# A two-attention kernel with a list scheduler: first weights through another DMA queue, constants later, smaller staging tiles, more output tiles, and new cost numbers

## The chip, the cores and the metric

The kernel runs on one core of a Trainium2 chip. The metric is the device time of one execution in microseconds (us), lower is better. Every number quoted as a time is the median of a kernel's fast runs; a kernel that is compared was run on the same chip as runs of the kernel before, alternating with them. The "span" of a profile is the time from the first to the last instruction of one profiled execution; it is about 2 us shorter than the time.

## The reference

Two attention layers on separate inputs of 2048 rows and 640 columns, with 32 heads of 20 columns each. The outputs stand side by side.

```python
def A(x, wq, wk, wv, wo, beta):         # 4 segments of 512 rows
    q, k, v = split_heads(x @ wq), split_heads(x @ wk), split_heads(x @ wv)
    g = sigmoid(beta)                   # one gate per head
    for s in range(4):
        p = softmax(qs @ ks.T * scale + causal_mask)      # inside the segment
        a_dot = p @ vs
        a_mem = (phi(qs) @ M) / (phi(qs) @ z + 1e-6)      # memory of earlier segments
        o = g * a_mem + (1 - g) * a_dot
        M, z = M + phi(ks).T @ vs, z + sum(phi(ks))
    return o @ wo                       # phi(t) = t + 1 if t > 0 else exp(t)

def B(x, wqkv, wo):                     # causal, window of 256 rows
    scores = where(0 <= i - j < 256, q @ k.T * scale, -1e9)
    return (softmax(scores) @ v) @ wo
```

## The kernel before

The work is cut into eight chunks of 512 rows, A0, B0, A1, B1, A2, B2, A3, B3. For each chunk there are projections (q, k, V), scores with an exponential on ScalarE, value products, a normalisation on VectorE, and a final projection with `wo`. This document numbers chunks and stages from 0 to 7; stage n runs from the end of the last score exponential of chunk n-1 to that of chunk n, and the tail runs from the end of the last score exponential to the end of the span.

The order of the instructions is fixed while the program is built, by a list scheduler written in Python. Class `Flow` keeps a modelled clock for each engine. A number such as `f.on_dve(607.0)` issues nothing: it only tells the scheduler how long the instruction just issued is believed to take. A changed cost number changes the order of the instructions and nothing else.

```python
class Flow:                                   # modelled clocks, ns
    def on_pe(self, mode, ns, ready=0.0): ...
    def on_dve(self, ns, ready=0.0):
        self.dve = max(self.dve, ready + 100.0) + ns
        return self.dve
    def when_idle(self, t, fn):               # VectorE work for when it is idle by the model
        self.idle_dve.append((t, fn))
...
def close(self, i, t):                        # one of two PSUM banks is free at modelled time t
    self.f.bank_free[i] = t
```

Projections of q and k are "bounced": TensorE's result is copied to a staging tile, stored to scratch memory in DRAM, and spread from there over the partitions of `qA`, `kA`, `qB` or `kB`. phi takes one exponential on ScalarE and two VectorE instructions, which are issued when the model sees VectorE idle.

```python
def qk_job(self, n, what, half, w_ap, scratch, dst, needs):
    ...                                       # 5 matmuls into a bank for each m
        nc.vector.tensor_copy(out=st[:, m, :], in_=ps[:, :])
        t = f.on_dve(615.0, f.pe)
        self.close(bi, t)
        self.bounce(m, st, scratch, dst, t, n, what)
...
def phi(self, out, in_, ready, then):
    e = self.wk.tile([P, L], BF16, name="e", bufs=2)
    nc.scalar.activation(out=e[:], in_=in_, func=ACT.Exp)
    ta = f.on_act(519.0, ready)
    def s1():
        nc.vector.tensor_single_scalar(out=e[:], in_=e[:], scalar=1.0, op=ALU.min)
        f.on_dve(200.0)
    def s2():
        nc.vector.scalar_tensor_tensor(out=out, in0=in_, scalar=0.0, in1=e[:],
                                       op0=ALU.max, op1=ALU.add)
        f.on_dve(650.0)
    f.when_idle(ta + 50.0, s1); f.when_idle(ta + 50.0, s2)
```

The final projection of a chunk loads the stored output transposed and does 8 groups of five matmuls (4 row blocks, two halves of the columns). There are 310 such matmuls in all, called *finals* below; the last row block of B3 goes another way.

```python
def final_job(self, n, o, scr, wo, out2d, r0, col, t0, t1):
    yield t
    yield self.quiet                          # not while a bounce is under way
    ...                                       # store o to scratch
    nc.sync.dma_start_transpose(out=oT[:, :, t0 * P:t1 * P], in_=scr[t0 * P:t1 * P, :])
    for tt in range(t0, t1):
        ot = self.wk.tile([P, 640], BF16, name="ot", bufs=2)
        for hf in range(2):
            yield "bank"
            ...                               # 5 matmuls, a VectorE copy to ot
        ...                                   # store ot to the output
```

The projections of a chunk are seeded as jobs when the scores of the chunk ahead of it begin. For chunk B1 they are seeded in two parts, and the argument `early` says which part takes V along:

```python
self.seed(n + 1, False if n == 2 else None)   # n: chunk whose scores begin now
if n == 1:
    self.seed(3, True)                        # B1's k early; its q follows with early=False
...
if early is not False:                        # in seed(): V goes with k
    add(self.v_job(n, half, *v))
```

The softmax here doesn't subtract the row's maximum and nothing guards it: scores larger than these inputs give would overflow.

## Time and profile before

| | before |
|---|---|
| time, median of 4 fast runs | 402.5 us (400.4 to 404.7) |
| span of the profiled run | 400.8 us |
| ScalarE / TensorE / VectorE busy | 337.7 / 348.7 / 318.7 us |
| first score exponential | 14.4 us |
| last score exponential ends | 383.6 us |
| tail | 17.2 us |

The page of the profile gives the sums (columns of its second line: busy us, share of the span, number of instructions) and, in 40 slices of the span, the granted TensorE clock (the share of full speed at which TensorE ran) in tenths:

```profile
span 400.8 us, 11055 instructions
...
PE 348.7 (87%) x4260; PEld 159.7 (40%) x4260; DVE 318.7 (80%) x654; ACT 337.7 (84%) x396; POOL 268.2 (67%) x552
...
PEclk9999999998999999999999999999999999999699
```

Three engines are busy 80 to 87% of the time, so which of them limits has to be read stage by stage.

The ScalarE timeline (start us, busy us, line, operation, count, and in brackets the idle time before it and what ended that) shows three gaps of the start:

```profile
14.38 5.61 ACT L568 ACTIVATE pt<-sc 128x1024 bf16<-128x1024 f32 x6 [6.89 <-PE sc L556]
...
29.46 20.37 ACT L568 ACTIVATE pt<-sc 128x1024 bf16<-128x1024 f32 x22 [4.11 <-PE sc L556]
...
70.68 18.15 ACT L568 ACTIVATE pt<-sc 128x768 bf16<-128x768 f32 x22 [3.00 <-PE sc L556]
```

The view of waits says that VectorE's copies to the output tile waited four times, 5.8 us in all, for a store to let the tile go:

```profile
DVE ot L784 <- DMA out_dram<-ot: 5.8, 4, 2.2
```

The TensorE timeline of the tail shows how finals run when nothing else is left: one group of five each 0.68 to 0.74 us, and one wait for the last transposed load.

```profile
391.32 0.84 PE L778 MATMUL m_7589<-wo_B,oT 128*128 128x320 bf16 x5
392.06 0.84 PE L778 MATMUL m_7596<-wo_B,oT 128*128 128x320 bf16 x5
395.49 0.85 PE L778 MATMUL m_7607<-wo_B,oT 128*128 128x320 bf16 x5 [2.58 <-DMA oT<-scr_o_216]
```

Finally, the groups of VectorE's instructions by form (busy us, mean ns of one, idle before) give the true length of what the scheduler believes. The trace's mean is after the bar and comma:

```profile
L588 DVE TENSOR_TENSOR pt<-pt,fdmask 128x512 bf16<-128x512 bf16 x64 | 29.9, 467 | 1.5 <-ACT pt L568 1.5
L688 DVE TENSOR_TENSOR u<-tt,rr 128x320 bf16<-128x320 f32 x24 | 15.0, 626 | 1.8
L387 DVE TENSOR_SCALAR e<-e 128x512 bf16<-128x512 bf16 x33 | 12.6, 382 | 0.0
L391 DVE SCALAR_TENSOR_TENSOR stq<-stq,e 128x512 bf16<-128x512 bf16 x15 | 11.8, 788 | 0.3
```

The kernel's numbers for these four are 350, 410, 200 and 650 ns. All are too low. The changed kernel has 440, 540, 300 and 740.

### The profile page before, as it was taken

The numbers are of one execution on the slowest core, as the hardware profiler recorded it, in microseconds if no ns is written. First come the engines' busy times: TensorE is split into PE (matmuls) and PEld (weight loads), VectorE is DVE, ScalarE is ACT, GpSimd is POOL, SyncE is SP. The second block draws the span as 40 slices with busy tenths as digits, with TensorE's granted clock in tenths as the row PEclk, the third lists the DMA queues.
The fourth block names the chain that finished last, engine by engine and source line by source line (L and its number), as shares of the span: only waits on it lengthen the run. The fifth ranks groups of instructions, "written<-read, shape, count | busy, mean of one in ns | idle before, by whom it ended". The sixth has DMA issues, their size and how long they took to land.

```text
span 400.8 us, 11055 instructions
## 1 busy us (share of the span) xinstructions
PE 348.7 (87%) x4260; PEld 159.7 (40%) x4260; DVE 318.7 (80%) x654; ACT 337.7 (84%) x396; POOL 268.2 (67%) x552
## 2 busy tenths in 40 slices
PE   6889999989898787798898988799789987998893
PEld 2334333434433323344443333344443334555462
DVE  6566699568998878977899988987778889988472
ACT  1549991989899998999999998999979998999820
POOL 5226660898867777988676786988756877756520
PEclk9999999998999999999999999999999999999699
DMA  7965255885438725152653925062526322237482
GB/s 170 283 255 175 74 139 146 196 205 140 104 101 208 149 86 127 48 150 88 150 110 115 231 84 136 13 165 80 154 73 167 96 70 69 77 108 147 107 179 83
DMA packets 101653, 52.67 MB, mean 131 GB/s; under 512 B 71712, under 2 KB 101536, under 8 KB 101536
## 3 DMA queue, kind: packets, MB, share of 16 engines
q1 hardware_dynamic: 101456, 51.88, 50.2%
q8 instruction: 33, 0.54, 0.6%
q14 instruction: 20, 0.16, 0.1%
q10 hardware_dynamic: 144, 0.08, 0.1%
HBM read 18.19 MB, written 23.10 MB: 103 GB/s over the span
## 4 chain that ended last, share of the span: by engine, by line
PE 35%; DVE 34%; ACT 10%; POOL 8%; DMA 6%; issue 6%; SPq 1%; ACTq 0%; DVEq 0%
ACT pt L568 10%; DVE tt L658 8%; PE sc L556 6%; POOL pt L606 4%; DVE o L688 3%; DVE st L367 3%; DVE ot L784 3%; DMA out_dram<-ot 2%; POOL pt L603 2%; DVE e L387 2%; PE m_73 L246 2%; DMA pkT<-scr_pk_197 2%; DVE stk L391 2%; DVE stq L391 2%; DVE rr L676 2%
## 5 line engine op out<-in xcount | busy, mean ns | idle before, releaser
L568 ACT ACTIVATE pt<-sc 128x1024 bf16<-128x1024 f32 (+1 forms) x360 | 322.4, 1016 | 34.1 <-PE sc L556 33.1
L606 POOL TENSOR_SCALAR_AFFINE_SELECT pt<-pt 128x256 bf16<-128x256 bf16 (+1 forms) x336 | 176.8, 536 | 107.4 <-ACT pt L568 105.3
L603 POOL TENSOR_SCALAR_AFFINE_SELECT pt<-pt 128x256 bf16<-128x256 bf16 x160 | 76.1, 479 | 7.7 <-ACT pt L568 7.4
L688 DVE TENSOR_TENSOR o<-tt,rr 128x320 bf16<-128x320 f32 x64 | 37.9, 592 | 1.9
L778 PEld LDWEIGHTS <-oT 128*128 128x128 bf16 x310 | 27.8, 98 | 25.7 <-issue 10.6
L556 PE MATMUL sc<-qA,kA 32*128 32x128 bf16 (+3 forms) x512 | 36.2, 301 | 2.1 <-ACT pt L568 1.6
L511 PEld LDWEIGHTS <-xT 128*128 128x128 bf16 x320 | 25.7, 97 | 27.7 <-issue 13.7
L588 DVE TENSOR_TENSOR pt<-pt,fdmask 128x512 bf16<-128x512 bf16 x64 | 29.9, 467 | 1.5 <-ACT pt L568 1.5
L556 PE MATMUL sc<-qB,kB_128 32*128 32x128 bf16 (+2 forms) x416 | 27.4, 270 | 1.8 <-ACT pt L568 1.8
L556 PE MATMUL sc<-qB,kB_129 32*128 32x128 bf16 (+1 forms) x480 | 25.1, 246 | 4.2 <-ACT pt L568 4.1
L556 PEld LDWEIGHTS <-kA 32*128 32x128 bf16 x512 | 10.9, 91 | 38.5 <-issue 36.6
L696 POOL TENSOR_TENSOR o<-o,u 128x320 bf16<-128x320 bf16 x24 | 19.6, 817 | 0.0
L556 PEld LDWEIGHTS <-kB_128 32*128 32x128 bf16 x416 | 10.0, 92 | 21.8 <-issue 20.4
L619 PEld LDWEIGHTS <-vA 128*32 128x32 bf16 x512 | 11.0, 96 | 18.3 <-DVE st L367 5.2
L556 PEld LDWEIGHTS <-kB_129 32*128 32x128 bf16 x480 | 10.5, 94 | 17.9 <-issue 16.9
L688 DVE TENSOR_TENSOR u<-tt,rr 128x320 bf16<-128x320 f32 x24 | 15.0, 626 | 1.8
L676 DVE RECIPROCAL rr<-tt 128x16 f32<-128x16 f32 x64 | 14.9, 234 | 0.3
L361 PEld LDWEIGHTS <-wBq 128*128 128x128 bf16 x100 | 8.8, 97 | 13.2 <-issue 5.3
L361 PEld LDWEIGHTS <-wBk 128*128 128x128 bf16 x100 | 8.5, 97 | 12.2 <-issue 4.9
L387 DVE TENSOR_SCALAR e<-e 128x512 bf16<-128x512 bf16 x33 | 12.6, 382 | 0.0
L391 DVE SCALAR_TENSOR_TENSOR stq<-stq,e 128x512 bf16<-128x512 bf16 x15 | 11.8, 788 | 0.3
L361 PEld LDWEIGHTS <-wq_A 128*128 128x128 bf16 x75 | 6.4, 97 | 10.9 <-issue 5.9
(666 smaller groups left out, 627.0 us busy)
## 6 DMA issues: line engine op xcount, KB each, us to landing
out_dram<-ot SPq DMA_DIRECT2D x31, 160.0 KB
wBk<-in_B_wqkv_dram SPq DMA_DIRECT2D x1, 800.0 KB
wBq<-in_B_wqkv_dram SPq DMA_DIRECT2D x1, 800.0 KB
wBv<-in_B_wqkv_dram SPq DMA_DIRECT2D x1, 800.0 KB
scr_wo_A<-in_A_wo_dram SPq DMA_DIRECT2D x4, 200.0 KB
wo_A<-scr_wo_A SPq DMA_DIRECT2D x1, 800.0 KB
scr_wo_B<-in_B_wo_dram SPq DMA_DIRECT2D x4, 200.0 KB
wo_B<-scr_wo_B SPq DMA_DIRECT2D x1, 800.0 KB
```

The lines of the kernel that those rows point to most:

```text
L361: nc.tensor.matmul(ps[:, :], lhsT=w_ap[:, kt, m * P:(m + 1) * P], rhs=xT[:, kt, :], start=(kt == 0), stop=(kt == self.KT - 1))
L391: nc.vector.scalar_tensor_tensor(out=out, in0=in_, scalar=0.0, in1=e[:], op0=ALU.max, op1=ALU.add)
L511: nc.tensor.matmul(ps[:, nw * x:nw * (x + 1)], lhsT=xT[:, kt, tt * P:(tt + 1) * P], rhs=w_ap[:, kt, DH * h0:DH * h0 + nw], start=(kt == 0) ...
L556: nc.tensor.matmul(ps[j // 2][:, j % 2, c0:c0 + nq * P], lhsT=k[rows, g, P * kc:P * kc + P], rhs=q[rows, g, q0 * P:(q0 + nq) * P], start=T ...
L568: nc.scalar.activation(out=pt[:, :, lo:hi], in_=ps[i][:, :, lo:hi], func=ACT.Exp, scale=self.scale)
L588: nc.vector.tensor_tensor(out=pt[:, :, 0:256], in0=pt[:, :, 0:256], in1=self.fd[:].unsqueeze(1).to_broadcast([P, 2, 256]), op=ALU.mult)
L603: nc.gpsimd.affine_select(out=blk, in_=blk, pattern=pat, compare_op=ALU.is_ge, fill=self.zero, base=-1, channel_multiplier=1)
L606: nc.gpsimd.affine_select(out=blk, in_=blk, pattern=pat, compare_op=ALU.is_ge, fill=self.zero, base=0, channel_multiplier=-1)
L658: self.nc.vector.transpose(out=tt[:, :], in_=O[:, :])
L676: nc.vector.reciprocal(out=rr[:], in_=src)
L688: nc.vector.tensor_tensor(out=to, in0=a, in1=b, op=ALU.mult)
L778: nc.tensor.matmul(ps[:, 0:320], lhsT=oT[:, m, tt * P:(tt + 1) * P], rhs=wo[:, m, 320 * hf:320 * hf + 320], start=(m == 0), stop=(m == sel ...
```

## The change

The intent has several parts. The first pieces of the first two weights and the gate `beta` are loaded through ScalarE's DMA queue instead of SyncE's. The gate constants leave VectorE's first path. Loads and stores on SyncE's queue wait, with a patience, while a bounce is under way. Chunks of B use five staging tiles of one piece each instead of two tiles of five pieces, and the output has four tiles instead of two. V of chunk B1 is projected with its q instead of with its early k (below: the *early flip*). And fourteen cost numbers of the scheduler are raised towards what instructions really take (below: the *cost numbers*). The diff, cut to its core (cuts are marked with dots; the comments in it are mine):

```diff
-        def part(i):
+        def part(i, eng=self.nc.sync):
...
-        part(0)
+        part(0, eng or self.nc.sync)                 # eng = ScalarE for wk_A and wq_A
...
-    def quiet(self):
+    def quiet(self, patience):
         f = self.f
-        return None if f.bouncing else max(0.0, f.sp)
+        end = f.pe + patience
+        return lambda: end if f.bouncing else max(0.0, min(f.sp, end))
...
-        t = f.on_dve(607.0, f.pe)                    # eviction of A0's k and q
+        t = f.on_dve(700.0, f.pe)
...
-        self.st[(n, what)] = self.st_tile("st" + what) if n % 2 == 0 else self.wk.tile(
-            [P, self.KT, L], BF16, name="st", bufs=2)
+        self.st[(n, what)] = self.st_tile("st" + what) if n % 2 == 0 else None
...
-            nc.vector.tensor_copy(out=st[:, m, :], in_=ps[:, :])
-            t = f.on_dve(615.0, f.pe)
+            to = st[:, m, :] if n % 2 == 0 else self.wk.tile([P, L], BF16, name="st", bufs=5)[:]
+            nc.vector.tensor_copy(out=to, in_=ps[:, :])
+            t = f.on_dve(670.0, f.pe)
...
-            f.on_dve(200.0)                          # phi, first instruction
+            f.on_dve(300.0)
-            f.on_dve(650.0)                          # phi, second instruction
+            f.on_dve(740.0)
...                                                   # more such: memory update 700 -> 1100,
...                                                   # V 75 + 1.04 n -> 120 + 1.08 n, mask 350 -> 440,
...                                                   # POOL mask 130 + 114 r -> 220 + 110 r,
...                                                   # transpose 640 -> 700, add 75 -> 220,
...                                                   # reciprocal 165 -> 210, multiply 410 -> 540,
...                                                   # POOL add 450 -> 750, final copy 405 -> 440
-        ot = self.wk.tile([P, 640], BF16, name="ot", bufs=2)
+        ot = self.wk.tile([P, 640], BF16, name="ot", bufs=4)
...
-            if early is not False:
+            if early is not True:
                 add(self.v_job(n, half, *v))
...
-        f.pe = f.act = 7000.0
+        f.pe = f.act = 4500.0
...
-            add(self.job(self.proj_direct(0, self.wk_A, self.xs[0], self.kA, g, "k", 6800.0)))
-            add(self.job(self.proj_direct(0, self.wq_A, self.xs[0], self.qA, g, "q", 6900.0)))
-            if g in (1, 5):
+            add(self.job(self.proj_direct(0, self.wk_A, self.xs[0], self.kA, g, "k", 5000.0)))
+            add(self.job(self.proj_direct(0, self.wq_A, self.xs[0], self.qA, g, "q", 5100.0)))
+            if g in (2, 5):
...
-        late = [self.consts_beta, self.consts_gates]
+        late = [self.consts_gates]                   # and only after 35 us instead of 12
...
-                n, g, what = pend[0]                 # value product or memory product
+                x = 0                                # skip memory products whose M is not ready
+                while x < len(pend) - 1 and pend[x][2] == "mem" and self.done.get(
+                        ("dm", chunks[pend[x][0]][1] - 1), 1e12) > f.pe:
+                    x += 1
+                n, g, what = pend[x]
```

## The prediction

> **What bounds it now.** By the page, ScalarE is busy 337.8 us of a 400.8 us span; TensorE 348.7, VectorE 318.7. The ScalarE timeline places the other 63 us: about 13 before its first exponential (14.4 us), 5.7 in two gaps (20.0 to 29.5), about 9 between 61 and 70.7, about 15 in some twenty gaps from 70 to 335, about 17 after its last exponential (383.6). So ScalarE bounds the middle, with TensorE and VectorE close behind, but not start and tail.
>
> **What the change does, by place.** Read from the built instruction order of both kernels.
>
> 1. First weights on ScalarE's queue: worth almost nothing. The first projection starts at 10.81 us, right behind 24 warm-up matmuls (3.13 to 10.75 us), which stay. First exponential still near 14.4.
> 2. Constants off the first path: VectorE's beta and gate constants, 16.85 to 20.0 us, delay V's evictions and stall TensorE 1.8 us; groups 2's q and k now also precede V. The gaps at 20 and 25 us mostly close. B's first scores stand about ten projection matmuls (2 us) earlier, and the qB spread no longer queues behind the 2 us of pk stores. First B score: 70.2 to about 65.5 us. Gain 5.
> 3. Four output tiles remove VectorE's 5.8 us of waits for output stores. ScalarE was covered for most of it: gain 2.
> 4. New order in the middle: all 310 final-projection matmuls move behind the first seven score stages (before, 120 ran within them), freeing about 17 us of TensorE and 11 us of VectorE there. Stages 1 to 6 hold only 15 us of ScalarE idle; expect 4 to 5 back. The last B chunk's q is finished later: lose about 1.
> 5. Tail: after the last score, 157 final matmuls remain instead of 52. Twenty-one more groups of five at 0.70 us (the undisturbed tail spacing) are 15 us. The chunk-6 transpose load is also queued on SyncE behind stores of chunk 5's last tiles; the large loads take 2.9 us to issue, and the small one landed 1.7 us after issue end, so TensorE waits about 4.5 us for it. (The Trainium skill, "DMA: Bandwidth & Descriptors", Anatomy of one DMA, gives about 2.0 us fixed for another queue path; 1.7 is near.) The tail, last score to end, was 18.8 us (382.0 to 400.8); estimate 38 (33 to 42).
>
> **Sum.** Last score from 382.0 to about 372; tail 38; span about 410; 2 us as now between span and time: 412 us.
>
> **What the profile would show.** First projection within 0.5 us of 10.8. No gate constants on VectorE before 20 us; ScalarE gaps at 20 to 30 us under 2 us in all. First B score at 64 to 67.5. No final-projection groups before the last chunk's scores. Waits of output copies for output stores near zero. Last score at 366 to 377. After it 31 final groups, ScalarE idle over 30 us, TensorE waiting 3 us or more once on a large transposed load.
>
> **What would make it wrong.** ScalarE idle in stages 1 to 6 nearly vanishing (another 8 us), a tail overlapping its loads better than the in-order SyncE queue suggests; or reused staging tiles making VectorE wait for stores. Even with no ScalarE idle between 14 us and the last score, a 36 us tail gives about 398, so over 2% faster is unlikely.
>
> 412 us, 8 in 10 within 402 to 420; faster 0.05, same 0.42, slower 0.53.

## More of the kernel before

The main loop takes at each modelled time a score batch if one is ready, else a value product, else the first job that can go. All projections stand in front of all finals:

```python
hit = None
for x, jb in enumerate(self.jobs + self.fins):
    t = self.need_time(jb[1])
    if t <= f.pe:
        hit = x
        break
```

The view of windows gives, for stages 2 to 5 and the tail: start:end, length, then the busy time and instructions of each engine, the granted clock, the DMA share and GB/s.

```profile
core 0: us, PE busy (x) PEld busy (x) DVE busy (x) ACT busy (x) POOL busy (x), PEclk, DMA share, GB/s
...
110.30:152.50 42.20, 35.36 (x364) 13.77 (x357) 36.25 (x75) 40.06 (x45) 30.54 (x57) 1.00 0.57 136
152.50:203.20 50.70, 44.87 (x543) 21.36 (x543) 43.21 (x91) 47.27 (x55) 40.33 (x81) 1.00 0.41 109
203.20:245.30 42.10, 37.36 (x378) 15.18 (x376) 38.11 (x79) 40.08 (x46) 31.99 (x56) 1.00 0.61 146
245.30:296.50 51.20, 44.38 (x542) 21.28 (x542) 42.57 (x89) 47.20 (x55) 40.24 (x81) 1.00 0.35 96
...
383.60:400.80 17.20, 10.45 (x117) 6.79 (x115) 7.50 (x17) 0.44 (x1) 0.95 (x2) 0.99 0.47 117
```

In the four middle stages ScalarE is idle only 2 to 4 us of 42 to 51, so ScalarE bounds the middle. It does not bound the start or the tail: in the tail it is busy 0.44 us.

Different sets of experiments ran on different chips, so it is the ratio to the kernel before, more than the bare time, that compares kernels of two sets.

## The result

| | before | after |
|---|---|---|
| time, median of fast runs | 402.5 us (400.4 to 404.7, 4 runs) | 428.4 us (427.7 to 431.8, 4 runs) |
| span of the profiled run | 400.8 us | 426.5 us |
| ScalarE / TensorE / VectorE busy | 337.7 / 348.7 / 318.7 us | 335.5 / 368.0 / 328.4 us |
| first B score on TensorE | 70.2 us | 64.9 us |
| last score exponential ends | 383.6 us | 384.6 us |
| tail | 17.2 us | 41.9 us |
| mean granted clock | 0.987 | 0.935 |

The ratio is 1.066, with a 95% interval of 1.058 to 1.074: the changed kernel is 6.6% slower. Here and below, a ratio is the mean time of one kernel's fast runs over that of the other's of the same rounds, so it is not quite the ratio of the quoted medians. The prediction, 412 us with 402 to 420 as the range, is missed.

The page after, the lines that answer to those shown of before:

```profile
span 426.5 us, 11104 instructions
...
PE 368.0 (86%) x4260; PEld 166.5 (39%) x4260; DVE 328.4 (77%) x651; ACT 335.5 (79%) x396; POOL 268.8 (63%) x552
...
PEclk9999999799996688999996987999999999999967
```

The same 4260 matmuls are busy 19 us longer, and the clock is below full speed in slices where it was full before. The windows of stages 2 to 5 and of the tail (columns as before):

```profile
102.80:151.10 48.30, 39.75 (x375) 14.06 (x374) 40.81 (x79) 42.61 (x52) 31.16 (x55) 0.86 0.43 106
151.10:197.60 46.50, 39.51 (x482) 17.31 (x481) 38.59 (x77) 44.38 (x50) 41.65 (x83) 0.93 0.41 102
197.60:249.30 51.70, 42.66 (x385) 16.40 (x384) 41.69 (x80) 42.44 (x52) 30.61 (x54) 0.90 0.34 91
249.30:295.30 46.00, 39.56 (x484) 18.30 (x484) 39.24 (x79) 44.38 (x50) 41.37 (x83) 0.93 0.41 106
...
384.60:426.50 41.90, 28.99 (x218) 18.43 (x217) 17.57 (x37) 0.45 (x2) 0.76 (x2) 0.86 0.56 143
```

All stages in one table, us, from the ScalarE timelines and these windows (ScalarE idle is the sum of the idle times that its timeline names in brackets):

| | 0 | 1 | 2 | 3 | 4 | 5 | 6 | 7 | tail |
|---|---|---|---|---|---|---|---|---|---|
| chunk | A0 | B0 | A1 | B1 | A2 | B2 | A3 | B3 | |
| before | 59.7 | 50.6 | 42.2 | 50.7 | 42.1 | 51.1 | 38.1 | 49.0 | 17.2 |
| after | 57.0 | 45.9 | 48.3 | 46.5 | 51.7 | 46.0 | 39.2 | 50.0 | 41.9 |
| difference | -2.7 | -4.7 | +6.1 | -4.2 | +9.6 | -5.1 | +1.1 | +1.0 | +24.7 |
| ScalarE idle, before | 18.6 | 12.5 | 2.1 | 3.1 | 1.9 | 3.7 | 0.6 | 2.8 | |
| ScalarE idle, after | 16.4 | 9.5 | 5.6 | 2.1 | 9.3 | 1.6 | 0.0 | 4.8 | |

So the start gained 7.4 us, stages 2 to 7 together lost 8.5, and the tail lost 24.7.

The start, in the ScalarE timeline: the gap ahead of 29.46 us has become 2.13 us, and the one ahead of 70.68 is now 1.61 us, at 65.34. The first exponential did not come sooner. A gap of 4.44 us is new, in the last chunk.

```profile
14.97 11.10 ACT L581 ACTIVATE pt<-sc 128x1024 bf16<-128x1024 f32 x12 [7.49 <-PE sc L569]
...
31.00 16.60 ACT L581 ACTIVATE pt<-sc 128x1024 bf16<-128x1024 f32 x18 [2.13 <-PE sc L569]
...
65.34 3.35 ACT L581 ACTIVATE pt<-sc 128x768 bf16<-128x768 f32 x4 [1.61 <-PE sc L569]
...
344.70 1.51 ACT L581 ACTIVATE pt<-sc 128x768 bf16<-128x768 f32 x2 [4.44 <-PE sc L569]
```

The waits of VectorE for output stores are gone from the view of waits (5.8 us before).

The tail, in the timeline of TensorE and of SyncE's queue (SPq):

```profile
401.12 0.84 PE L791 MATMUL m_7520<-wo_B,oT 128*128 128x320 bf16 x5
401.73 2.84 SPq L783 DMA_TRANSPOSE oT<-scr_o_226  x1
...
406.63 1.51 PE L791 MATMUL m_7538<-wo_A,oT 128*128 128x320 bf16 x5 [4.67 <-DMA oT<-scr_o_226]
407.94 1.54 PE L791 MATMUL m_7545<-wo_A,oT 128*128 128x320 bf16 x5
...
411.85 0.84 PE L791 MATMUL m_7569<-wo_A,oT 128*128 128x320 bf16 x5
...
418.68 1.51 PE L791 MATMUL m_7620<-wo_B,oT 128*128 128x320 bf16 x5 [2.40 <-DMA oT<-scr_o_227]
```

The transposed load of A3's output is issued at 401.73, when TensorE has just done its last group that was ready; TensorE stands 4.67 us. After that wait a group takes 1.5 instead of 0.84 us for four groups, and again after the wait of 2.40 us.

Why is more left for the tail? The instruction order can be counted without running anything. This table gives matmuls of the built order by stage (here a stage begins with the first score matmul of its chunk), with the last column after the last score:

| | 0 | 1 | 2 | 3 | 4 | 5 | 6 | 7 | after |
|---|---|---|---|---|---|---|---|---|---|
| finals, before | 0 | 0 | 5 | 48 | 17 | 48 | 2 | 138 | 52 |
| finals, after | 0 | 0 | 0 | 0 | 0 | 0 | 0 | 153 | 157 |
| A's q and k, before | 0 | 50 | 0 | 50 | 0 | 50 | 0 | 0 | 0 |
| A's q and k, after | 0 | 50 | 0 | 30 | 20 | 43 | 7 | 0 | 0 |
| A's V, before | 40 | 40 | 0 | 40 | 0 | 40 | 0 | 0 | 0 |
| A's V, after | 40 | 2 | 38 | 18 | 22 | 20 | 20 | 0 | 0 |

Before, all projections of A1, A2 and A3 are done while the chunk ahead is scored, and the finals fill what is left. After, a part of them slips into the chunk's own stage: V of A1 nearly whole, of A2 20 of 50 matmuls for q and k and 22 of 40 for V, of A3 7 and 20. As long as there is a backlog of projections, no final runs, because finals stand last in the list.

What such a slip does can be read in stage 4 (chunk A2, from 197.6). The spreads of A2's k on SyncE's queue, first of the kernel before (stage 4 starts at 203.2 there), then of after:

```profile
176.12 1.43 SPq L337 DMA_DIRECT2D kA<-scr_kA_195  x4
192.00 1.61 SPq L337 DMA_DIRECT2D kA<-scr_kA_195  x4
```

```profile
190.86 1.44 SPq L348 DMA_DIRECT2D kA<-scr_kA_206  x4
211.71 1.46 SPq L348 DMA_DIRECT2D kA<-scr_kA_206  x4
```

Before, the second half of k leaves 11.2 us ahead of the stage; after, 14.1 us into it. Without those keys only half of the head groups can be scored. In the TensorE timeline of after there is no A2 score between 211.6 and 220.3; TensorE does projections of B2 meanwhile. ScalarE shows it:

```profile
217.07 0.63 ACT L394 ACTIVATE e<-stk 128x512 bf16<-128x512 bf16 x1 [1.69 <-DVE stq L402]
220.83 3.77 ACT L581 ACTIVATE pt<-sc 128x1024 bf16<-128x1024 f32 x4 [3.14 <-PE sc L569]
...
227.10 0.63 ACT L394 ACTIVATE e<-stk 128x512 bf16<-128x512 bf16 x1 [1.18 <-DVE stk L402]
```

Two things sit here: the scores that come late (3.14 us; they stand behind the projections of B2 in TensorE's order), and phi's exponentials of the late k. Those wait for VectorE to free one of the two tiles `e` (1.69 and 1.18 us), and the score exponentials behind them on ScalarE wait too. The Trainium skill, "TensorE: Matmul & The Clock Gate", section "Architectural detail", says that ScalarE's and VectorE's queues are strictly first in, first out, which is what this trace shows.

### The profile page after: what moved, and what is told of

The parts are those of the page before. It is cut to its first block, busy times and chain, and to the rows that moved or that the text cites. A ratio compares the mean times of both kernels' runs of the same rounds, so it can differ in the third digit from the quotient of the medians.

```text
span 426.5 us, 11104 instructions
## 1 busy us (share of the span) xinstructions
PE 368.0 (86%) x4260; PEld 166.5 (39%) x4260; DVE 328.4 (77%) x651; ACT 335.5 (79%) x396; POOL 268.8 (63%) x552
## 4 chain that ended last, share of the span: by engine, by line
PE 47%; DVE 20%; ACT 18%; issue 7%; DMA 5%; SPq 2%; POOL 1%; ACTq 0%; DVEq 0%
ACT pt L581 17%; PE sc L569 9%; DVE tt L671 4%; DVE o L701 2%; PE m_73 L247 2%; DVE st L378 2%; DVE pt L601 1%; DVE u L701 1%; ACT e L394 1%; DVE e L398 1%; DVE rr L689 1%; DMA oT<-scr_o_226 1%; DVE stk L402 1%; DMA qA<-scr_wo_B 1%; POOL pt L619 1%
## 5 line engine op out<-in xcount | busy, mean ns | idle before, releaser
L619 POOL TENSOR_SCALAR_AFFINE_SELECT pt<-pt 128x256 bf16<-128x256 bf16 (+1 forms) x336 | 178.9, 541 | 112.6 <-ACT pt L581 110.3
L569 PE MATMUL sc<-qA,kA 32*128 32x128 bf16 (+3 forms) x512 | 41.5, 318 | 12.8 <-ACT pt L581 11.9
L791 PEld LDWEIGHTS <-oT 128*128 128x128 bf16 x310 | 30.0, 103 | 24.8 <-DMA oT<-scr_o_226 5.0
L524 PEld LDWEIGHTS <-xT 128*128 128x128 bf16 x320 | 26.1, 101 | 27.4 <-issue 17.1
L569 PE MATMUL sc<-qB,kB_126 32*128 32x128 bf16 (+2 forms) x416 | 30.8, 275 | 6.1 <-ACT pt L581 5.4
L601 DVE TENSOR_TENSOR pt<-pt,fdmask 128x512 bf16<-128x512 bf16 x64 | 31.2, 497 | 0.4
L569 PE MATMUL sc<-qB,kB_127 32*128 32x128 bf16 (+1 forms) x480 | 26.9, 245 | 3.5 <-ACT pt L581 3.1
L569 PEld LDWEIGHTS <-kB_126 32*128 32x128 bf16 x416 | 11.4, 92 | 29.2 <-issue 27.7
L569 PEld LDWEIGHTS <-kB_127 32*128 32x128 bf16 x480 | 11.5, 92 | 17.8 <-issue 16.3
L701 DVE TENSOR_TENSOR u<-tt,rr 128x320 bf16<-128x320 f32 x24 | 13.4, 559 | 1.2
L247 PE MATMUL m_73<-qB 128*128 128x512 bf16 x24 | 8.2, 523 | 3.1 <-DVE qB L906 3.1
```

The lines of the kernel that those rows point to most:

```text
L524: nc.tensor.matmul(ps[:, nw * x:nw * (x + 1)], lhsT=xT[:, kt, tt * P:(tt + 1) * P], rhs=w_ap[:, kt, DH * h0:DH * h0 + nw], start=(kt == 0) ...
L569: nc.tensor.matmul(ps[j // 2][:, j % 2, c0:c0 + nq * P], lhsT=k[rows, g, P * kc:P * kc + P], rhs=q[rows, g, q0 * P:(q0 + nq) * P], start=T ...
L601: nc.vector.tensor_tensor(out=pt[:, :, 0:256], in0=pt[:, :, 0:256], in1=self.fd[:].unsqueeze(1).to_broadcast([P, 2, 256]), op=ALU.mult)
L619: nc.gpsimd.affine_select(out=blk, in_=blk, pattern=pat, compare_op=ALU.is_ge, fill=self.zero, base=0, channel_multiplier=-1)
L701: nc.vector.tensor_tensor(out=to, in0=a, in1=b, op=ALU.mult)
L791: nc.tensor.matmul(ps[:, 0:320], lhsT=oT[:, m, tt * P:(tt + 1) * P], rhs=wo[:, m, 320 * hf:320 * hf + 320], start=(m == 0), stop=(m == sel ...
```

## The experiments

The theory after the comparison: the loss is all in the order, the tail because 157 finals are left, stages 2 and 4 because projections slip past their stage. Who moved them? Two parts of the change can alter the order of the middle, the early flip and the cost numbers. The rivals: the tail is long because of its loads or its clock, not because of the number of finals; stages 2 and 4 are long because of phi's tiles and the low clock, or because banks are booked longer. Eighteen kernels were run; all gave the reference's result, filler matmuls included. The expectation is printed ahead of each result. In e1, e3, e4, e5, e9 and e11 to e15 the time came out above the first range that the expectation names.

In the lists below, "finals left" are the final matmuls after the last score in the built order; the tail, stages 2 + 4 and the end of the last score exponential are in us, from each run's profile. The before kernel has 52, 17.2, 84.3, 383.6; after has 157, 41.9, 100.0, 384.6.

### First set: which part, and what if finals went first

**e1: the whole change without the early flip.**

```diff
-            if early is not True:
+            if early is not False:
```

> The whole change except one line, the test that decides which projections of the second B chunk are seeded early (early is not False, as before). In the built order 130 of the 310 final-projection matmuls stand again before the last chunk's scores, and 43 instead of 157 stand after the last score. Theory D (the loss is the deferral of the final projections): tail back to 18 to 22 us from 43.6, TensorE clock 0.97 or more again, time 392 to 404 us. Rival R (the new staging, bounce order or start part are slow by themselves): stays at 415 us or more.

Measured: 406.6 us, ratio 1.009 (1.004 to 1.015). Finals left 43, tail 17.2, stages 2 + 4 90.8, last exponential 387.1. The tail is back, but stage 3 is 66.3 us long with one gap on ScalarE:

```profile
168.15 33.13 ACT L581 ACTIVATE pt<-sc 128x1024 bf16<-128x1024 f32 x36 [19.73 <-PE sc L569]
```

It follows that the number of finals left goes with the tail, and that the early flip, with these cost numbers, gets rid of a 20 us gap in stage 3 but pays for it at the end. In this order 45 finals run in stage 3 and 56 in stage 2.

**e2: the whole change without the cost numbers.** All on_dve and on_pool numbers back, nothing else:

```diff
-            f.on_dve(300.0)          # phi; and likewise all the other cost numbers
+            f.on_dve(200.0)
```

> The whole change except the generator's new cost numbers for VectorE and GpSimd work. 115 final-projection matmuls stand before the last chunk, 53 after the last score. Theory D: 392 to 405 us, tail 18 to 24 us. Rival R: 415 us or more. A second rival, that the early flip is bad in itself and not only together with the costs, expects e1 fast and e2 still above 412.

Measured: 395.9 us, ratio 0.983 (0.978 to 0.987). Finals left 53, tail 19.2, stages 2 + 4 86.5, last exponential 374.3. Stage 4, the tail, and the second spread of A2's k:

```profile
197.20:238.60 41.40, 36.97 (x372) 15.12 (x376) 36.95 (x79) 40.09 (x45) 32.60 (x56) 1.00 0.61 146
...
374.30:393.50 19.20, 11.79 (x115) 7.11 (x113) 7.09 (x15) 0.44 (x1) 0.77 (x2) 0.91 0.45 109
```

```profile
185.39 1.44 SPq L348 DMA_DIRECT2D kA<-scr_kA  x4
```

So the cost numbers, in the presence of the rest, cost 428.4 - 395.9 = 32.5 us (medians of different rounds; the ratios, 1.066 and 0.983, say the same): 22.7 in the tail and 13.5 in stages 2 and 4, with about 3.7 returned elsewhere. The k of A2 leaves 11.8 us ahead of stage 4 again.

**e3: the changed kernel with finals ahead of projections.**

```diff
-            for x, jb in enumerate(self.jobs + self.fins):
+            cand = self.fins + self.jobs
+            for x, jb in enumerate(cand):
...
-                jb = (self.jobs + self.fins)[hit]
+                jb = cand[hit]
```

> The changed kernel with one rule altered: the generator offers a free bank to final projections before other projections. 240 final matmuls then stand before the last chunk, 11 after the last score. Theory D: tail 17 to 21 us, time 390 to 406. Rival R: 415 or more. If instead the final projections in the middle push back the next chunk's projections, gaps of ScalarE at the chunk borders, over 3 us each, eat part of it.

Measured: 438.2 us, ratio 1.086 (1.080 to 1.092). Finals left 11, tail 15.6, but the last exponential ends at 421.4, with 14.8, 15.7, 11.5 and 12.8 us of ScalarE idle in stages 2, 3, 4 and 6. The tail is as short as one could wish and the kernel is slower still. A final ahead of a projection is only free if the projection can wait, and here it cannot.

**e4: the start part alone, on the kernel before** (weights on ScalarE's queue, constants, order of A0's projections).

```diff
-        f.pe = f.act = 7000.0
+        f.pe = f.act = 4500.0       # with all other start lines of the change
```

> The start part alone on the kernel before: first weights and beta by ScalarE's queue, gate constants early or late, V after group 2, start times of the model. Tail count 21 final matmuls. Expected from the trace of the change: first exponential at 14.4 to 15.0 us (no gain there), first B score 4 to 5 us earlier; with the tail as before the time is 394 to 400 us. If moving the weights mattered, the first exponential would come before 13.5 us.

Measured: 404.1 us, ratio 1.004 (0.996 to 1.011). Stages 0 + 1 take 103.2 instead of 110.3, the gain that the start was meant to bring. But stage 3 is 59.5 with 10.7 us of ScalarE idle, and the finals left are 21. The start part gains 7 us at its place, and the scheduler, which starts from other clocks, makes another middle and gives them back.

### Second set: tiles, clock, and the costs alone

**e5: after with four tiles `e`.** The theory called K has the cost numbers lengthen stages 2 and 4 through phi: two tiles, stalls of ScalarE, and then a lower clock. The built order does not change on any engine.

```diff
-        e = self.wk.tile([P, L], BF16, name="e", bufs=2)
+        e = self.wk.tile([P, L], BF16, name="e", bufs=4)
```

> The changed kernel with four instead of two tiles e for the exponentials of phi; every engine's instruction order is the same as in the changed kernel. It takes away the waits of those exponentials (ScalarE, in front of the next score exponentials) for VectorE. Theory K: these waits start a chain, ScalarE blocked, the next score matmul held 3 us, TensorE's clock halved for some us, scores late. Then the stall of 3.2 us in stages 2 and 4 goes, the clock there rises from 0.86 and 0.90 to 0.97 or more, both stages together lose 6 to 12 us, and the time is 414 to 422 us. Rival O (the new instruction order starves ScalarE by itself): within 4 us of the changed kernel's 428.

Measured: 425.7 us, ratio 1.058 (1.050 to 1.065). Tail 41.9, stages 2 + 4 99.2. TensorE's waits in stage 2, the longest one of the changed kernel first and then those of e5 (columns: us in total, times, longest):

```profile
PE sc L569 <- ACT pt L581: 3.2, 1, 3.2
```

```profile
PE m L632 <- POOL pt L619: 2.4, 1, 2.4
PE m L632 <- DVE tt L671: 2.2, 2, 1.6
...
PE sc L569 <- ACT pt L581: 1.1, 1, 1.1
```

The wait for a score exponential shrank from 3.2 to 1.1 us, and the waits of value products for VectorE's transposes (`tt`) grew from 0.6 to 2.2 us; the 2.4 us for GpSimd stood in the changed kernel too. ScalarE's idle time in stages 2 and 4 stayed (5.5 and 9.0 us, against 5.6 and 9.3). The tile part of theory K falls.

**e6: after with useless matmuls that bridge the tail's two waits** (24 ahead of the first final group of A3, 12 ahead of the last ones of B3). They write into a bank that the group overwrites.

```diff
                 ps, bi = self.bank()
+                fill = (24 if n == 6 else 12 if n == 7 and t0 == 1 else 0) if tt == t0 and hf == 0 else 0
+                for _ in range(fill):
+                    nc.tensor.matmul(ps[:, :], lhsT=self.wk_A[:, 0, 0:P], rhs=self.wk_A[:, 0, 0:L],
+                                     start=True, stop=True)
```

> The changed kernel with 24 matmuls of no use ahead of the first final group of chunk 6 and 12 ahead of the second tile of chunk 7, in the bank that the group then overwrites; they keep TensorE busy during the two waits for transposed loads. If the half-speed matmuls after these waits (four groups at 1.33 us, three at 1.3, against 0.73) come from the wait, they return to 0.73 us and the tail falls from 43.6 us after the last score to 39 to 40. If the clock falls by something else (load, chance), the tail stays or grows.

Measured: 423.9 us, ratio 1.054 (1.046 to 1.062); tail 38.6 (40.4 from the last score). In the TensorE timeline the filler (`wk_A`) stands where the wait was, and the eight groups behind it (40 matmuls) take 5.78 us, 0.72 each:

```profile
393.56 5.84 PE L795 MATMUL m<-wo_B,oT 128*128 128x320 bf16 x40
399.30 5.34 PE L792 MATMUL m<-wk_A 128*128 128x512 bf16 x23
404.48 5.78 PE L795 MATMUL m<-wo_A,oT 128*128 128x320 bf16 x40
```

The clock in the tail rose from 0.86 to 1.00. So 3.3 us of the tail (41.9 - 38.6) are matmuls at half speed, and it is TensorE's standing idle in the waits that brings them: with the waits filled they are gone. The remaining 21 us of loss in the tail are something else.

**e7: e2 with four tiles `e`.**

```diff
-        e = self.wk.tile([P, L], BF16, name="e", bufs=2)
+        e = self.wk.tile([P, L], BF16, name="e", bufs=4)
```

> All of the change but the cost numbers (the second run of the first series, 395.9 us), with four tiles e. Its ScalarE waits 4.4 us and 1.6 us for phi tiles, the longer one at the border to the first B chunk, where scores wait for their own loads anyway. Theory K: 391 to 395 us; rival O: 395 to 397.

Measured: 394.8 us, ratio 0.982 (0.975 to 0.988), finals left 53, tail 19.6, stages 2 + 4 86.7. No different from e2.

**e8: the cost numbers alone, on the kernel before.**

```diff
-            f.on_dve(200.0)
+            f.on_dve(300.0)          # and all the other cost numbers
```

> The new cost numbers alone on the kernel before. 80 final matmuls before the last chunk, 78 after the last score (52 before). If the costs are the harmful part by themselves: 412 to 420 us, a tail of 22 to 25 us after the last exponential, clock in stages 2 and 4 under 0.95. If they do harm only together with the early flip: 400 to 408.

Measured: 414.1 us, ratio 1.030 (1.020 to 1.039). Finals left 78, tail 29.8, stages 2 + 4 82.6, stage 3 58.4 with a gap of 10.6 us. So the cost numbers alone lengthen the tail, but not stages 2 and 4. What stages 2 and 4 suffer in the changed kernel needs the cost numbers and another part together. (A2's k leaves 10 us ahead of stage 4 here.)

### Third set: the clock, the start, and the best version

**e9: after with four useless matmuls ahead of each value product of stages 2 and 4**, to raise the clock there.

```diff
-    def av(self, parts, g, vof):
+    def av(self, parts, g, vof, fill=0):
         O, bi = self.bank()
+        for _ in range(fill):                 # 4 in chunks A1 and A2
+            nc.tensor.matmul(O[:, :], lhsT=self.wk_A[:, 0, 0:P], rhs=self.wk_A[:, 0, 0:L],
+                             start=True, stop=True)
```

> The changed kernel with four 512-column matmuls of no use ahead of each value product of stages 2 and 4, in the bank that the product then overwrites (16 products, 14 us of work at 0.21 us each). Theory K (the low clock of stages 2 and 4, 0.86 and 0.90, is what makes them 48.3 and 51.7 us long): clock there 0.97 or more, both stages together 4 to 8 us shorter in spite of the added work, time 418 to 424 us. Rival O (the stages are long because of the order of the work and VectorE; the low clock only accompanies it): the clock may rise, but the two stages stay within 3 us or grow, time 426 to 434.

Measured: 434.2 us, ratio 1.077 (1.071 to 1.084), stages 2 + 4 105.1. Stage 4:

```profile
200.60:253.50 52.90, 45.30 (x397) 18.21 (x403) 40.79 (x80) 42.83 (x51) 29.25 (x54) 0.97 0.34 89
```

The clock rose from 0.90 to 0.97 (in stage 2 from 0.86 to 0.93) and the stages got no shorter. ScalarE's idle time did not shrink. But the filler is some 14 us of TensorE work by itself, so the run does not price the clock. The trace of the changed kernel says more about stage 4. These are two windows of it:

```profile
210.00:222.00 12.00, 11.15 (x93) 4.56 (x90) 10.27 (x19) 7.18 (x11) 4.07 (x8) 1.00 0.42 127
222.00:235.00 13.00, 8.99 (x64) 2.78 (x62) 10.43 (x23) 10.41 (x13) 7.79 (x14) 0.74 0.34 77
```

ScalarE's longest idle time of the stage (3.14 us) and one of 1.69 fall into the first, at full clock, so the low clock did not make them; it comes afterwards. In the other 4.4 us of ScalarE's idle time in stage 4 it may have a part, and so it may in stage 2; that is not shown either way.

**e10: without the cost numbers and without the early flip.**

```diff
-            if early is not True:
+            if early is not False:
```

> All of the change but the costs and the early flip. 35 final matmuls after the last score, 130 before the last chunk. In both kernels so far that had the old early rule beside the new start part, ScalarE waited long at the border to the second B chunk (19.7 us; 10.7 us in all), because that chunk's q was projected last. If the flip is what closes this gap: a gap of 6 to 12 us in stage 3 and 400 to 408 us. If the gap comes from the other parts: 392 to 397 us as with the flip.

Measured: 393.4 us, ratio 0.977 (0.970 to 0.983), the best of all. Finals left 35, tail 12.6, stages 2 + 4 85.3, last exponential 378.3. Against e2 the tail is 6.6 us shorter and stage 3 is 7.3 us longer, where 63 finals run now and one gap stands:

```profile
152.34 3.88 ACT L581 ACTIVATE pt<-sc 128x1024 bf16<-128x1024 f32 x4 [6.83 <-PE sc L569]
```

So without the cost numbers the early flip is an even exchange: e2 and e10 don't differ by more than their intervals. Both beat the kernel before, by about 2%; whether by more than 2% the interval leaves open.

**e11: e2 without the start part.**

```diff
-        f.pe = f.act = 4500.0       # with all other start lines
+        f.pe = f.act = 7000.0
```

> All of the change but the costs and the start part. 70 final matmuls after the last score. The start part shortened stage 0 to the first B score by 4 to 7 us in every run that had it; if that time survives to the end, this run is 4 to 7 us slower than the 395.9 us with it, 400 to 403 us; if later stages absorb it, 395 to 398.

Measured: 410.2 us, ratio 1.018 (1.011 to 1.025). Finals left 70, tail 27.4, stages 2 + 4 88.6. The start part is worth 14 us in this company and nothing alone (e4). Stages 0 and 1 take 104.0 us here, where the kernel before took 110.3: e2's other parts bring most of that gain without the start part, as the start part did without them (103.2). Parts of such a change cannot be added up.

**e12: e2 with finals first during chunks B1 and B2.** In e2 the stages of B1 and B2 hold the most finals of the middle, 48 each.

```diff
+            cand = self.fins + self.jobs if started in (3, 5) else self.jobs + self.fins
```

> All of the change but the costs, and final projections offered free banks first in the stages of chunks 3 and 5 alone. 210 final matmuls before the last chunk, 20 after the last score (53 without). If finals in those stages cost nothing there (TensorE 44.9 of 49.9 us busy, VectorE 43.8), the time is 389 to 393 us. If they displace the next chunk's projections or fill VectorE, stage 3 grows by over 5 us and the time is 396 us or more.

Measured: 417.8 us, ratio 1.036 (1.031 to 1.041). Finals left 20, tail 16.6, but stage 4 64.5 with a gap of 13.5 us. In the built order 120 finals run in stage 3, and half of A2's V slips into stage 4. The second spread of A2's k leaves at 212.2 us, 17 us into the stage.

### Fourth set: banks

**e13: after, with banks offered 700 ns earlier.** Theory B: higher cost numbers make the scheduler believe that banks come free later, so it offers them to fewer jobs. Only the model's belief changes; the real wait stays in the program, so it is free of races.

```diff
     def close(self, i, t):
-        self.f.bank_free[i] = t
+        self.f.bank_free[i] = t - 700.0
```

> The changed kernel, costs and flip kept, but the generator takes an accumulator bank to be free 0.7 us before its modelled VectorE read ends (the hardware still waits for the real read). Projections then stand in their old stages, 110 final matmuls before the last chunk, 70 after the last score. Theory B (the longer costs let the generator offer banks too rarely; the projection backlog never empties and crowds out the finals): 396 to 408 us, tail after the last exponential 21 to 26 us instead of 41.9, stages 2 and 4 together 86 to 92 us instead of 100. If the longer costs do harm in another way (placement of masks, norms, phi), stages 2 and 4 stay above 96 us and the time above 412.

Measured: 429.1 us, ratio 1.064 (1.059 to 1.068). Finals left 70, tail 30.6; stage 4 44.7, but stage 2 56.7 with a gap of 8.0 us. Theory B holds for the order and not for the time: banks offered earlier clear the backlog (70 finals left instead of 157, and A2's k 7.6 us ahead of its stage), and stage 4 returns, but stages 2 to 7 together grew by 11.7 us against the changed kernel, stage 2 most, which takes back all that the tail gained.

**e14 and e15: e10 with banks 150 and 300 ns earlier.** Can the best version be pressed further?

```diff
-        self.f.bank_free[i] = t
+        self.f.bank_free[i] = t - 150.0      # e15: 300.0
```

> The best so far (all but the costs and the early flip, 393.4 us) with banks taken to be free 0.15 us earlier: 160 final matmuls before the last chunk, 20 after the last score instead of 35. By theory B with room left in TensorE and VectorE: 388 to 392 us. If the middle is full already, finals moved there lengthen it by what the tail loses: 392 to 397.

> As the run before it with 0.3 us: 175 final matmuls before the last chunk, 19 after the last score. Same expectation, 388 to 394 us; over 396 us would mean that TensorE now waits in order for banks that VectorE has not freed, and holds up scores behind them.

Measured: 405.4 us (ratio 1.004, 1.000 to 1.008) and 405.0 us (1.003, 0.998 to 1.008). Finals left 20 and 19, last exponentials at 384.1 and 390.0. More finals go into the middle, and the last exponential ends 6 to 12 us later. Both expectations missed. ScalarE was not out of time there: its idle time in stages 2 to 7 grew from 18.2 us in e10 to 22.9 and 27.5. TensorE's waits for VectorE between the end of stage 1 and the last exponential grew from 20.1 us to 30.3 in e14 (to 23.7 in e15, with 4.0 more for transposed loads), which fits TensorE standing in order before banks that are not free yet; it is not shown that this is all.

### Fifth set: which cost numbers

The changed kernel with one group of cost numbers at its old values each time.

**e16: phi's two numbers.**

```diff
-            f.on_dve(300.0)
+            f.on_dve(200.0)
...
-            f.on_dve(740.0)
+            f.on_dve(650.0)
```

> The changed kernel with the two phi cost numbers of before. 118 final matmuls after the last score. If the tail is set by their number, the line through the second run (53 finals, 19.2 us after the last exponential) and the changed kernel (157, 41.9) gives 33 us, and 30 to 37 counts as agreement. If the placing of phi by its costs is what lengthens stages 2 and 4 (100 us together), they fall below 93 us and the time below 414; if not, they stay above 96.

**e17: normalisation and memory update.**

```diff
-            f.on_dve(1100.0)       # memory update; also 220 -> 75, 210 -> 165,
+            f.on_dve(700.0)        # 540 -> 410, POOL add 750 -> 450
```

> The changed kernel with the norm, GpSimd-add and memory-update costs of before. 125 finals after the last score: tail 35 us by the same line (31 to 39). If these costs lengthen stages 2 and 4, those fall below 93 us and the time below 416; otherwise they stay above 96.

**e18: evictions, transposes, V and masks.**

```diff
-            t = f.on_dve(670.0, f.pe)      # also 700 -> 607, V, masks,
+            t = f.on_dve(615.0, f.pe)      # transpose 700 -> 640, final copy 440 -> 405
```

> The changed kernel with the eviction, transpose and mask costs of before. 93 finals after the last score: tail 28 us by the line (25 to 32). If these costs lengthen stages 2 and 4, those fall below 93 us and the time below 408; otherwise they stay above 96.

| | e16 phi | e17 norm | e18 evictions | after | e2 all old |
|---|---|---|---|---|---|
| time, us | 403.5 | 410.6 | 400.9 | 428.4 | 395.9 |
| ratio to before | 0.999 | 1.017 | 0.991 | 1.066 | 0.983 |
| 95% interval | 0.991 to 1.007 | 1.010 to 1.023 | 0.984 to 0.999 | 1.058 to 1.074 | 0.978 to 0.987 |
| finals left | 118 | 125 | 93 | 157 | 53 |
| tail | 34.0 | 33.3 | 28.0 | 41.9 | 19.2 |
| stage 1 | 51.8 | 45.8 | 44.5 | 45.9 | 44.6 |
| stage 2 | 42.3 | 49.4 | 46.6 | 48.3 | 45.1 |
| stage 4 | 41.3 | 44.1 | 42.2 | 51.7 | 41.4 |
| A2's k leaves, from start of stage 4 | -2.2 | -2.5 | +0.2 | +14.1 | -11.8 |

Any one group taken back brings stage 4 to 41 to 44 us. No single group is to blame: the last step of the backlog, that which carries A2's k deep into its own stage, needs all three. (e17's stages 2 and 4, 93.5 us, fall between the two expectations, since its stage 2 stayed long.) phi's two numbers give stages 2 and 4 back altogether (83.6), but take 5.9 us in stage 1.

### What the set shows together

*The tail.* A line through e2 (53 finals, 19.2 us) and after (157, 41.9) has 0.22 us for each final, 1.1 us for each group of five. Of that, 0.72 us is the spacing of undisturbed groups in the timeline; I take the rest to be the waits and the half clock, spread over all groups. The line puts e16 at 33.4, e17 at 34.9 and e18 at 27.9; measured 34.0, 33.3 and 28.0. It puts e8, e11 and e13 4 to 8 us too low (29.8, 27.4, 30.6 with 70 to 78 finals left), so it is a rule of thumb, not a law. With 35 finals or fewer the tail is 11 to 18 us whatever their number. That the finals left make the tail is shown; the rival "clock" is worth 3.3 us (e6), and the rival "loads" was not tested apart: TensorE's waits for loads in the tail sum to 9.2 us in the changed kernel (2.15, 4.67 and 2.40) and to 2.6 before, and they are inside the line.

*Stage 4.* In every kernel run whose stage 4 is over 50 us, the second spread of A2's k leaves 5 us or more after the stage has begun: after, e5, e6 and e9 (one order), e3 (5.8 us into the stage; stage 54.4) and e12 (17 us; 64.5). In all others it leaves ahead of the stage or with its start, and the stage takes 41 to 45 us. With the gap and the phi waits in the trace of after this is a strong reading. It is still a reading: no run moved A2's k alone, and V of A2 slips along with it.

*Stage 2* is not settled. It is 42 us where most of A1's V is done in stage 1 (before, e8), and 45 us or more in most kernels where it falls into stage 2, but e16 has 29 of 40 there with 42.3 us and e4 has 20 with 46.5. So a part of what stage 1 gained may only have gone to stage 2 with A1's V; no run separates this.

## Why the prediction was wrong

1. *Step 1, weights on ScalarE's queue worth almost nothing.* Right. The first exponential came at 14.97 us (before 14.38), and over all profiles of this case at 13.4 to 15.0, whatever the kernel. The first projection was at 11.41 us, just outside "within 0.5 of 10.8": the warm-up ran to 11.35.
2. *Step 2, constants off the first path, gain 5.* Right. The first B score was at 64.9 us (predicted 65.5). The gate constants were not on VectorE before 20 us. The gaps at 20 to 30 us were 0.85 and 2.13, 3.0 us in all where under 2 was named (the second ends at 31.0).
3. *Step 3, four output tiles, gain 2.* The 5.8 us of waits are gone, as predicted. With the start, stages 0 and 1 gained 7.4 us. In e4 and e11 either the start part or the rest alone gains 6 to 7 us there, so gains of steps 2 and 3 do not simply add; no run separates the tiles' share.
4. *Step 4, "all 310 final-projection matmuls move behind the first seven score stages ... Stages 1 to 6 hold only 15 us of ScalarE idle; expect 4 to 5 back. The last B chunk's q is finished later: lose about 1."* **This step failed.** Its count of finals was right: none ran before 342.8 us. In stages 3 and 5, where 48 finals each had run, the expected gain came and was larger than said, 4.2 + 5.1 = 9.3 us. But the step took the rest of the middle as unchanged, and it was not: the same built order that moves finals out has a part of A's projections late, in their own stage. Stages 2 and 4 grew by 6.1 + 9.6 us, stage 6 by 1.1 and the last stage by 1.0 (with a gap of 4.4 us on ScalarE). In the step's own terms, ScalarE's idle time between the first B score exponential and the end of stage 6 was to fall by 4 to 5 us; it rose from 15.6 to 21.7. Net, stages 2 to 7 lost 8.5 us where the step said a gain of 3 to 4; the last score on TensorE was at 382.9 instead of 372. The table of matmuls by stage, of which I had read only the row of the finals, showed the slip before any run. e2 and e16 to e18 showed that the cost numbers make it, together with the rest (e8). That A2's late k is what lengthens stage 4 is the reading of the traces; what lengthens stage 2 stays open.
5. *Step 5, tail 38.* The mechanism was right: 31 groups after the last score, one wait of over 3 us for a large transposed load (4.67 predicted as 4.5), ScalarE idle. The size was off: 43.6 us from the last score to the end, outside 33 to 42. Two terms were missing from the sum, 3.3 us of matmuls at half speed behind the waits (e6), and a wait of 2.15 us for the last weights, 5.4 us of the 5.6. (The wait of 2.40 us for the last load was not missing: the tail of before, from which the sum starts, has one of 2.58.) The estimate took all 21 added groups at the spacing of the undisturbed tail.
6. *What would make it wrong.* I named an idle-free middle, a tail overlapping better, and waits for reused staging tiles. All but the last were ways to be faster than 412 us, and none of the three came (VectorE waited for no transfer). That the middle may get slower was not on the list.

In sum: 382.9 instead of 372 is 11 us, 43.6 instead of 38 is 5.6 us; 412 + 11 + 5.6 = 428.6, and 428.4 was measured.

## What to carry to other kernels

When a change touches the numbers or the starting clocks of a list scheduler, it is a change of the whole order: count every kind of work by stage in both orders, above all the work that a stage must have *before* it starts, and not only the kind that you expect to move. Lowest-priority work runs only when the backlog ahead of it is empty; a little pessimism everywhere keeps the backlog alive, and all of the leftover lands where nothing can hide it. More truthful cost numbers are not in themselves a better schedule: here the rest of the change was worth about 2% with all of them taken back (e2), and under 1% with one group taken back (e18).

## What the Trainium skill lacked or had wrong

- "TensorE: Matmul & The Clock Gate", table of the two clock states, has half speed after an idle window of about 3.4 us, with a window that runs free. Half speed came here after a wait of 4.67 us, but also after one of 2.40 us (groups of 1.5 instead of 0.84 us), while a wait of 2.58 us in the kernel before was followed by a group of 0.85 us. So the plain figure is no safe limit for a single wait: one of 2.4 us can cost half speed too. Why one did and the other did not is not shown.
- The same page, section "HAM oscillation", puts the cost in long idle gaps. I found no page that says how to tell in a trace whether a clock below full speed (0.86 and 0.90 in stages 2 and 4) makes a stage long or follows from its idle times. Here the order of time helps: in stage 4 ScalarE's longest idle time (3.14 us) came at clock 1.00, and 0.74 came after it. Raising the clock to 0.93 and 0.97 with filler (e9) shortened nothing, though the filler's own time hides a part of what it gave.
- "DMA: Bandwidth & Descriptors", section "Anatomy of one DMA", gives about 2.0 us fixed, for GpSimd's path. For transposed loads on SyncE's queue the first matmul came 2.06 us after the end of the issue (401.73 + 2.84 to 406.63) for the large one. What that section has no figure for is the issue of such a load, 2.84 us for the large one, which is longer than the fixed part.
- I found no page that warns that in a list scheduler cost numbers nearer to the trace can make the kernel slower: 428.4 us with them, 395.9 without.
